# Two column chunks of wr and wi in one load, and another order of the first ten microseconds

## The chip, the core and the metric

The kernel runs on one core of one Trainium2 chip. A core has five engines that run their own instruction queues and wait for one another through semaphores: TensorE (matmuls and transposes into eight accumulator banks, in the profile PE, its weight loads PEld), VectorE (DVE), ScalarE (ACT), GpSimd (POOL) and SyncE (SP), whose queue here issues nearly all DMAs between the main memory and the on-chip memory of 128 partitions. The metric is the time of one execution on the device, in microseconds (us).

## The reference

x is 2048 x 640. It is normalised by row, xn = (x - mean) / sqrt(var + eps). Two branches of xn are summed with x:

```python
a = einsum("bsd,ed->bse", xn, wr)        # hidden DFT, 640 x 640, real part
b = einsum("bsd,ed->bse", xn, wi)        # imaginary part
y = einsum("ts,bse->bte", cr, a) - einsum("ts,bse->bte", ci, b)   # sequence DFT, 2048 x 2048
h = gelu(xn @ w1 + b1)                   # 640 -> 1536, tanh form
out = x + y + (h @ w2 + b2)              # 1536 -> 640
```

All matrices are inputs in float32, the DFT matrices too.

## The kernel before

Each matrix that goes through the TensorE is split into a high part, rounded to the type that the TensorE takes at full rate, and a low part, the rest. A product is then three matmuls, high by high, high by low, low by high (`product`, L278 to L280). `split` (L160, L161) makes the two parts: a copy on ScalarE, a subtraction on VectorE.

The rows of x are taken in four blocks of 512 (four chunks of 128 rows each). For the first block the MLP runs in twelve groups, one for each 128 columns of w1 (chunks of w1): `hidden(g)` gives 15 matmuls of 128x512 (five column chunks of x by three, L304), `gelu` and a split follow, and `output(g)` gives 15 matmuls into five banks, two groups later. The second block does the same beside the preparation of what follows; from about 180 us on blocks three and four of the MLP and then the sequence and hidden DFTs run, with sums and differences of operands that save products. The DFT matrices are turned on VectorE (32x32 transposes) after they are loaded, as the TensorE needs them the other way round.

The order of the instructions on each engine is the order in which the code is written; no scheduler changes it. A DMA of the SP queue uses one of eight semaphores in turn, so it also waits until the DMA eight places before it has landed. A tile of a pool with one buffer makes its next user wait for the readers of the last.

The front, up to the first products: x's first four chunks (0 to 3 in the code and here; the prediction counts them one to four) come by DMA. Meanwhile the TensorE runs ten warm-up matmuls on zeros (L676). Chunks 0 and 2 get their means on VectorE and are centred there (`center`, L705). Chunk 1 is summed (L699) and centred (L716) on ScalarE. Chunk 3 is summed on ScalarE and centred on VectorE, in two pieces, the first two column chunks and the other three. The centred chunks are turned on the TensorE (`transpose_x`, L693), five transposes each, into five banks, one for each column chunk of x; chunks 0 and 1 first, then one more warm-up, then chunks 2 and 3 by column chunk. Then the five banks are split into `XT` (in the profile xtt), the moving operand, the first chunk of w1 having been split in two pieces (L728, L729) before. The scale of the normalisation is made later and applied after the products: the TensorE spreads it over the columns with four transposes (`spread`, L764) one product into the third group.

wr and wi are needed in seven combinations of their column chunks, which are made, split and stored to memory (the wit tiles) long before their use. Column chunk j of one of them is the 32 columns j of each quarter of its columns, so a load of it (`load_w`, L388, four DMAs) has rows of 32 floats. `turn_w` (L396) turns a chunk; `put_w` splits and stores. `prep_w` does this in three steps for each chunk, beside the groups of the second block: chunk 0 in groups 0 to 2, chunk 1 in groups 3 to 5, the others from a later stage on. The names in the profile are wraw (as loaded), wt (turned), wst (split).

Of the kernel before, what the change touches and what calls it, by code (L numbers as in the profile page):

```python
# [16 lines left out]
Q = 4  # L17
B = 32
EPS = 1e-5
NWARM = 10  # L20
TAIL = 4
ASIDE = 1
PADL = 8
# [3 lines left out]
def kernel(  # L27
# [78 lines left out]
    def bank(k):  # L106
        return banks[:, k]
# [140 lines left out]
    def load_w1(i, eng=nc.sync, cuts=(0, ND)):  # L248
        if i >= NF:
            return  # L250
        t = early.tile([P, ND, P], F32, tag="w1r", bufs=3, name=f"w1r{i}")
        w1r[i] = t
        v = w1.rearrange("(q c i) f -> q i c f", q=Q, i=B)
        for c0, c1 in zip(cuts, cuts[1:]):
            for q in range(Q):
                eng.dma_start(t[q * B : (q + 1) * B, c0:c1], v[q, :, c0:c1, i * P : (i + 1) * P])
# [30 lines left out]
    def unit(g):  # L287
        return g if g < NF else LATE[g % NF]

    def hidden(g, aside=None):  # L290
# [4 lines left out]
        if g == 0:  # L295
            steps = FIRST
        if g == 1:

            steps.sort(key=lambda s: s[1] == 2)
        for n, (j, k) in enumerate(steps):  # L300
            if aside and n == ASIDE:
                aside()
            a, b = kinds[k]
            nc.tensor.matmul(  # L304
                acc, W1[i][:, a, j * P : (j + 1) * P], XT[j][:, b], start=n == 0, stop=n == len(steps) - 1
            )
        return acc


    FIRST = [(0, 0), (0, 2), (1, 0), (1, 2), (0, 1), (2, 0), (2, 2), (1, 1), (3, 0), (3, 2)]  # L310
    FIRST += [(2, 1), (4, 0), (4, 2), (3, 1), (4, 1)]

    def gelu(g, acc, fill=lambda k: None):

# [60 lines left out]

    A = {}

    def load_w(m, j):

        if A["w"]:  # L380
            t = A["w"].tile([P, EB, B], F32, tag=f"wraw{m}", bufs=1, name=f"wraw{m}_{j}")
        else:
            t = A["wz"][:, m].rearrange("p (e b) -> p e b", b=B)
        A["wraw", m] = t
        v = (wr, wi)[m].rearrange("(n r) d -> r n d", r=B)
        for q in range(Q):
            s0 = q * DQ + j * B
            nc.sync.dma_start(t[q * B : (q + 1) * B], v[:, :, s0 : s0 + B])  # L388

    def turn_w(m, j):  # L390
        if A["w"]:
            t = A["w"].tile([P, D], F32, tag=f"wt{m}", bufs=1, name=f"wt{m}_{j}")
        else:
            t = A["wz"][:, 2 + m]
        A["wt", m] = t
        nc.vector.transpose(  # L396
            t.rearrange("p (c q i) -> p q c i", q=Q, i=B),
            A.pop(("wraw", m)).rearrange("p (q c) i -> p q c i", q=Q),
        )
# [20 lines left out]
    def prep_w(s):  # L420

        j, k = divmod(s, 3)
        if j >= ND:
            return
        if k == 0:
            turn_w(0, j)
            turn_w(1, j)
            if j + 1 < ND and j != WEARLY - 1:
                load_w(0, j + 1)
                load_w(1, j + 1)  # L430
        (r1, r2, r4), (i1, i2, i4) = (
            (A["wt", m][:, : 2 * P], A["wt", m][:, 2 * P : 4 * P], A["wt", m][:, 4 * P :]) for m in range(2)
        )
# [12 lines left out]
        if k == 2:  # L446
            put_w(3, j, r1)
            put_w(4, j, i1)
            put_w(5, j, r2)
# [215 lines left out]
    nc.vector.memset(zeros, 0.0)  # L665
    warm = whole["as"][:, :TB]
    nc.vector.tensor_copy(warm, zeros)  # L667

    nc.scalar.activation(eps[:, 1:2], eps[:, 0:1], AF.Sqrt)
    load_w1(0, cuts=(0, 2, ND))  # L670
    load_w1(1, cuts=(0, 2, ND))

    wacc = bank(0)

    def warm_up():
        nc.tensor.matmul(wacc, warm[:, :P], warm, start=True, stop=True)  # L676

    for k in range(NWARM):
        warm_up()
    load_w1(2)  # L680
    load_w2(0)
    nc.sync.dma_start(b1c, b1.rearrange("(i p) -> p i", p=P))
    load_w2(1)
# [7 lines left out]
    def transpose_x(c, j0, j1):  # L691
        for j in range(j0, j1):
            nc.tensor.transpose(tacc[j][:, c * P : (c + 1) * P], xp[:, c, j * P : (j + 1) * P], ident)  # L693
# [32 lines left out]
    for lo, hi in ((0, 2 * P), (2 * P, D)):  # L726
        h, l = (W1[0][:, k, lo:hi] for k in range(2))
        nc.scalar.activation(h, first_w1[:, lo:hi], AF.Copy)  # L728
        nc.vector.tensor_tensor(l, first_w1[:, lo:hi], h.bitcast(F32), op=ALU.subtract)  # L729
    transpose_x(0, 0, ND)  # L730
# [202 lines left out]
    def first_block(i):  # L933

        if i < 2:
            ln_apply(2 * i)
            ln_apply(2 * i + 1)
            load_x(4 + 2 * i)
            load_x(5 + 2 * i)
        if 2 <= i < 6:  # L940
            ln_stats(4 + i - 2)
        if i == 6:
            ln_scale(4, 4)
            for c in range(4, 8):
# [24 lines left out]

    def open_tw():  # L970
        A["es"].close()
# [12 lines left out]
    def second_block(i):  # L984
# [816 lines left out]
```

## Time and profile before

| | |
|---|---|
| median of three runs | 851.04 us (850.51 to 851.35) |
| the profiled execution | 850.46 us, span 848.7 us |
| TensorE busy | 841.7 us of the span, 3707 matmuls |
| VectorE busy | 666.8 us |
| ScalarE busy | 356.0 us |
| first warm-up matmul | 1.91 us after the span's start |
| first product of the first block | 9.66 us |
| first matmul of the third group | 16.7 us |
| output 0 | 20.59 us |

A row of the profile's order of time has the start, the length, the engine, the line, the operation, what it writes and reads, the shape and the count of merged instructions; in brackets stands how long the engine had been idle before and who ended that. "SPq" and "ACTq" are DMAs issued by these queues; their length is that of the issue, not of the transfer. A row of the chain has the start, the length and what ran. A matmul's length in the profile includes its way through the array, so 0.39 us stands for a product of which one is started every 0.227 us. A row of waits has the engine and line that waited, whom it waited for, the sum, the count and the longest.

### The profile page before, as it was taken

To read this page: it belongs to the slowest core of one execution; us is meant where nothing else is said; L and a number is where in the kernel's file an instruction comes from. 1 tells how busy PE (TensorE), PEld (TensorE's weight loads), DVE (VectorE), ACT (ScalarE), POOL (GpSimd) and SP (SyncE) were. 2 spreads that over 40 slices of the span, in tenths; PEclk is the share of its full clock that TensorE was granted. 3 is DMA by queue.
4 is the path that set the end of the run, shared out by engine and by line. 5 is a ranking of instruction groups with operands and counts; after the bars stand their busy time and mean duration, and the time that the engine had idled before them with its cause. 6 is when DMAs were issued, how large, how long until landed. Compare 5 with 4: busy or idle time off the path is not lost.

```text
span 848.7 us, 10340 instructions
## 1 busy us (share of the span) xinstructions
PE 841.7 (99%) x3707; PEld 695.2 (82%) x3707; DVE 666.8 (79%) x841; ACT 356.0 (42%) x499; POOL 48.9 (6%) x70
## 2 busy tenths in 40 slices
PE   9999999999999999999999999999999999999997
PEld 7888888878888888888888888888888888888886
DVE  6665766776758888779988887889967898885687
ACT  7454534456665555343444344232323433223241
POOL 0000311031221400000000000000000000000001
PEclk9999999999999999999999999999999999999999
DMA  6667699837679989858644679663865779705464
GB/s 182 192 184 188 159 228 252 193 87 189 202 245 355 358 186 174 173 132 188 152 137 111 162 229 289 151 150 98 205 168 169 253 191 229 306 19 180 124 172 108
DMA packets 207491, 158.45 MB, mean 187 GB/s; under 512 B 81040, under 2 KB 180880, under 8 KB 206928
## 3 DMA queue, kind: packets, MB, share of 16 engines
q1 hardware_dynamic: 198752, 135.25, 62.7%
q0 software_dynamic: 4144, 21.24, 6.3%
q10 hardware_dynamic: 4544, 1.31, 0.6%
q8 instruction: 29, 0.48, 0.3%
q14 instruction: 22, 0.18, 0.1%
HBM read 114.76 MB, written 42.99 MB: 186 GB/s over the span
## 4 chain that ended last, share of the span: by engine, by line
PE 99%; DVE 0%; issue 0%
PE banks L278 29%; PE banks L279 29%; PE banks L280 29%; PE banks L304 10%; PE banks L676 1%; PE banks L693 0%; PE banks L336 0%; PE banks L339 0%; PE banks L337 0%; DVE yo L1766 0%; DVE zeros L665 0%; DVE as L667 0%; PE banks L764 0%
## 5 line engine op out<-in xcount | busy, mean ns | idle before, releaser
L278 PE MATMUL banks<-as,xab 128*128 128x512 f32 x411 | 159.9, 389 | 0.0
L280 PE MATMUL banks<-as,xab 128*128 128x512 f32 x411 | 159.9, 389 | 0.0
L279 PE MATMUL banks<-as,xab 128*128 128x512 f32 x411 | 159.9, 389 | 0.0
L160 ACT ACTIVATE as<-r 128x1024 fp32r<-128x1024 f32 x80 | 85.0, 1062 | 178.1 <-PE banks L280 149.7
L161 DVE TENSOR_TENSOR as<-r,as 128x1024 fp32r<-128x1024 f32 x80 | 97.2, 1216 | 41.5 <-ACT as L160 41.5
L278 PEld LDWEIGHTS banks<-as,xab 128*128 128x128 f32 x411 | 77.1, 188 | 16.1
L279 PEld LDWEIGHTS banks<-as,xab 128*128 128x128 f32 x411 | 77.1, 188 | 16.0
L280 PEld LDWEIGHTS banks<-as,xab 128*128 128x128 f32 x411 | 77.1, 188 | 16.0
L278 PE MATMUL banks<-as,xc 128*128 128x512 f32 x224 | 87.1, 389 | 0.0
L279 PE MATMUL banks<-as,xc 128*128 128x512 f32 x224 | 87.1, 389 | 0.0
L280 PE MATMUL banks<-as,xc 128*128 128x512 f32 x224 | 87.1, 389 | 0.0
L160 ACT ACTIVATE as<-rt 128x1024 fp32r<-128x1024 f32 x32 | 34.0, 1062 | 70.5 <-PE banks L280 62.5
L304 PE MATMUL banks<-xtt,xab 128*128 128x512 f32 x240 | 57.1, 391 | 0.0
L304 PEld LDWEIGHTS banks<-xtt,xab 128*128 128x128 f32 x240 | 44.7, 188 | 9.8 <-ACT xtt L160 0.4
L278 PEld LDWEIGHTS banks<-as,xc 128*128 128x128 f32 x224 | 42.0, 188 | 8.8
L279 PEld LDWEIGHTS banks<-as,xc 128*128 128x128 f32 x224 | 42.0, 188 | 8.7
L280 PEld LDWEIGHTS banks<-as,xc 128*128 128x128 f32 x224 | 42.0, 188 | 8.7
L161 DVE TENSOR_TENSOR as<-rt,as 128x1024 fp32r<-128x1024 f32 x32 | 38.8, 1211 | 5.3 <-ACT as L160 5.3
L160 ACT ACTIVATE as<-u 128x1024 fp32r<-128x1024 f32 (+1 forms) x24 | 22.1, 920 | 48.2 <-PE banks L280 48.2
L512 DVE STREAM_TRANSPOSE r<-raw 128x1024 f32<-128x1024 f32 x32 | 39.5, 1240 | 3.1 <-PE banks L280 2.6
L161 DVE TENSOR_TENSOR as<-u,as 128x1024 fp32r<-128x1024 f32 (+1 forms) x24 | 24.9, 1042 | 18.8 <-ACT as L160 18.8
L512 DVE STREAM_TRANSPOSE rt<-raw 128x1024 f32<-128x1024 f32 x32 | 38.8, 1230 | 0.9 <-PE banks L280 0.8
(352 smaller groups left out, 1618.5 us busy)
## 6 DMA issues: line engine op xcount, KB each, us to landing
raw<-in_A_dft_seq_re_dram SPq DMA_DIRECT2D x64, 256.0 KB, 5.6
raw<-in_A_dft_seq_im_dram SPq DMA_DIRECT2D x64, 256.0 KB, 5.0
ws<-wit SPq DMA_DIRECT2D x15, 384.0 KB, 5.4
xs<-x SPq DMA_DIRECT2D x64, 80.0 KB, 1.8
xo<-in_A_x_dram SPq DMA_DIRECT2D x16, 320.0 KB, 6.7
xab<-wit SPq DMA_DIRECT2D x13, 384.0 KB, 4.2
wit<-wstp POOLq DMA_DIRECT2D x12, 384.0 KB, 3.7
x<-in_A_x_dram SPq DMA_DIRECT2D x14, 320.0 KB, 4.4
```

Source lines behind the costliest of these rows:

```text
L160: nc.scalar.activation(h, s, AF.Copy)
L161: nc.vector.tensor_tensor(l, s, h.bitcast(F32), op=ALU.subtract)
L278: nc.tensor.matmul(acc, wh, mh, start=first, stop=False, skip_group_check=goes_on)
L279: nc.tensor.matmul(acc, wh, ml, start=False, stop=False, skip_group_check=goes_on)
L280: nc.tensor.matmul(acc, wl, mh, start=False, stop=last, skip_group_check=goes_on)
L304: nc.tensor.matmul(acc, W1[i][:, a, j * P : (j + 1) * P], XT[j][:, b], start=n == 0, stop=n == len(steps) - 1)
L512: nc.vector.transpose(held(pieces[g][2], u).rearrange("p c (n i) -> p c n i", i=B), r.rearrange("p n (c i) -> p c n i", i=B))
L676: nc.tensor.matmul(wacc, warm[:, :P], warm, start=True, stop=True)
```

## The change

There are two parts.

In the front, the warm-ups become thirteen matmuls of 128x128 on zeros in plain float32, so the cast of the zeros goes and the memset shrinks to 128 columns. The first two column chunks of x's chunk 3 are centred on ScalarE, right after the sum; chunk 2 is centred in two pieces. The split of w1's first 256 columns stands between the pieces, the split of the other 384 behind the first two copies of `XT`. Seven of chunk 2's and 3's ten transposes are done ahead of the first two products, the last three behind them. The first and second groups' products are mixed at their seam (`first_two`), and the order within each is another. w1's chunk 1 comes by four DMAs instead of eight, chunk 2 by eight instead of four.

wr's and wi's column chunks 0 and 1 are loaded together (`load_two`), with rows of 64 floats: the first 16 of wi's 20 row blocks go to a tile that lies idle (ZT), in the first block's group 10, before the stores of x that stand there; the other four of wi's and all of wr's follow at the place where chunk 0 was loaded. `turn_two` turns a chunk, wi's in three pieces and wr's in two, chunk 1 at the start of group 3 of the second block, ahead of the turning of z. The loads of chunk 1 at the end of group 0 go.

TensorE, from its first instruction to the third group, before (L676 are warm-ups, L693 transposes of x, L304 products of groups one and two, and with xab_123 of the third; L764 the spread):

```order
L676 MATMUL banks<-as 128x512 x10
L693 MATMUL banks<-ident,xp 128x128 x10
L676 MATMUL banks<-as 128x512
L693 MATMUL banks<-ident,xp 128x128 x10
L304 MATMUL banks<-xtt,xab_122 128x512 x30
L304 MATMUL banks<-xtt,xab_123 128x512
L764 MATMUL banks<-ident,ab 128x128 x4
```

The same after:

```order
L714 MATMUL banks<-zeros 128x128 x13
L731 MATMUL banks<-ident,xp 128x128 x10
L714 MATMUL banks<-zeros 128x128
L731 MATMUL banks<-ident,xp 128x128 x7
L304 MATMUL banks<-xtt,xab_122 128x512 x2
L731 MATMUL banks<-ident,xp 128x128 x3
L304 MATMUL banks<-xtt,xab_122 128x512 x28
L322 MATMUL banks<-xtt,xab_123 128x512
L810 MATMUL banks<-ident,ab 128x128 x4
```

Three transposes have moved behind the first two products, and the warm-ups have another shape and count.

ScalarE from the sum of chunk 3 (x_120) on, before (xab_122 holds w1's chunks 0 and 1 split, w1r their raw tiles):

```order
L699 ACTIVATE ab,mv<-x_120 128x640
L728 ACTIVATE xab_122<-w1r_139 128x256
L728 ACTIVATE xab_122<-w1r_139 128x384
L160 ACTIVATE xtt<-banks 128x512 x5
L160 ACTIVATE xab_122<-w1r_148 128x640
```

And after:

```order
L737 ACTIVATE ab,mv<-x_120 128x640
L767 ACTIVATE xp<-x_120,mv 128x4x2x32
L764 ACTIVATE xab_122<-w1r_138 128x256
L160 ACTIVATE xtt<-banks 128x512 x2
L764 ACTIVATE xab_122<-w1r_138 128x384
L160 ACTIVATE xtt<-banks 128x512 x3
L160 ACTIVATE xab_122<-w1r_147 128x640
```

The centring (L767) has come in ahead of w1, and w1's 384 columns stand behind two of the copies.

The SP queue from the load of xo on, 87 to 140 us, before (xs is x normalised, stored for the DFTs; ys and xo belong to the first block's output; z is the second block's operand; the last number of wraw's shape is the floats in a row):

```order
L363 DMA xo_842<-in_A_x_dram 32x16x160 x4
L203 DMA xs<-x_657 32x640 x4
...
L178 DMA x_879<-in_A_x_dram 128x640
L388 DMA wraw_0_919<-in_A_dft_hid_re_dram 32x20x32 x4
L388 DMA wraw_0_924<-in_A_dft_hid_im_dram 32x20x32 x4
L930 DMA ys_60<-xo_842 2048x1x64
L930 DMA ys_61<-xo_842 2048x1x64
L930 DMA ys_62<-xo_842 2048x1x32
L234 DMA z_1018<-xs 32x16x160 x4
L388 DMA wraw_1_1033<-in_A_dft_hid_re_dram 32x20x32 x4
L388 DMA wraw_1_1038<-in_A_dft_hid_im_dram 32x20x32 x4
L203 DMA xs<-x_873 32x640 x4
```

And after:

```order
L381 DMA xo_845<-in_A_x_dram 32x16x160 x4
L404 DMA zt<-in_A_dft_hid_im_dram 32x16x64 x4
L203 DMA xs<-x_660 32x640 x4
...
L178 DMA x_886<-in_A_x_dram 128x640
L404 DMA wrest<-in_A_dft_hid_im_dram 32x4x64 x4
L404 DMA wraw<-in_A_dft_hid_re_dram 32x10x64 x8
L976 DMA ys_60<-xo_845 2048x1x64
L976 DMA ys_61<-xo_845 2048x1x64
L976 DMA ys_62<-xo_845 2048x1x32
L234 DMA z_1029<-xs 32x16x160 x4
L203 DMA xs<-x_880 32x640 x4
```

Four loads have gone ahead of the stores of x, twelve stand where eight stood, and the eight behind the load of z are gone.

```diff
-NWARM = 10
+NWARM = 13
...
+    def first_two():
+        kinds = ((0, 0), (0, 1), (1, 0))
+        second = sorted(((j, k) for j in range(ND) for k in range(3)), key=lambda s: s[1])
+        order = [(0, s) for s in FIRST[:13]] + [(1, s) for s in second[:2]]
+        order += [(0, FIRST[13]), (1, second[2]), (0, FIRST[14])] + [(1, s) for s in second[3:]]
+        for n, (g, (j, k)) in enumerate(order):
+            if n == 2:
+                transpose_x(3, 2, ND)
+                for e in range(2, ND):
+                    split(XT[e][:, 0], XT[e][:, 1], tacc[e])
+                prep_w1(1)
...
+    def load_two(m, k0=0):
+        v = (wr, wi)[m].rearrange("(n r) d -> r n d", r=B)
+        for t, n0, n1 in TWO[m][k0:]:
+            for q in range(Q):
+                nc.sync.dma_start(t[q * B : (q + 1) * B], v[:, n0:n1, q * DQ : q * DQ + 2 * B])
+    def turn_two(m, j):
+        t = A["wt", m] = A["w"].tile([P, D], F32, tag=f"wt{m}", bufs=1, name=f"wt{m}_{j}")
...
-        if k == 0:
+        if k == 0 and j == 0:
+            turn_two(1, j)
+            turn_two(0, j)
+        if k == 0 and j >= WEARLY:
             turn_w(0, j)
             turn_w(1, j)
-            if j + 1 < ND and j != WEARLY - 1:
+            if j + 1 < ND:
...
-    nc.vector.memset(zeros, 0.0)
-    warm = whole["as"][:, :TB]
-    nc.vector.tensor_copy(warm, zeros)
+    nc.vector.memset(zeros[:, :P], 0.0)
...
-    load_w1(1, cuts=(0, 2, ND))
+    load_w1(1)
...
-        nc.tensor.matmul(wacc, warm[:, :P], warm, start=True, stop=True)
+        nc.tensor.matmul(wacc[:, :P], zeros[:, :P], zeros[:, :P], start=True, stop=True)
...
-    load_w1(2)
+    load_w1(2, cuts=(0, 2, ND))
...
-    center(2, ALU.subtract, MV[:, 2, 0:1])
     sum_on_act(3)
-    center(3, ALU.add, MV[:, 3, 5:6], 0, 2)
-    center(3, ALU.add, MV[:, 3, 5:6], 2, ND)
...
+    nc.scalar.activation(
+        chunked(xp[:, 3])[:, :, :2],
+        xt[3].rearrange("p (q c i) -> p q c i", q=Q, i=B)[:, :, :2],
+        AF.Identity,
+        bias=MV[:, 3, 5:6],
+    )
+    center(2, ALU.subtract, MV[:, 2, 0:1], 0, 2)
+    center(2, ALU.subtract, MV[:, 2, 0:1], 2, ND)
+    split_first(0, 2 * P)
+    center(3, ALU.add, MV[:, 3, 5:6], 2, ND)
     transpose_x(0, 0, ND)
     transpose_x(1, 0, ND)
     warm_up()
-    for j0, j1 in ((0, 2), (2, ND)):
-        transpose_x(2, j0, j1)
-        transpose_x(3, j0, j1)
-    for j in range(ND):
+    transpose_x(2, 0, 1)
+    transpose_x(3, 0, 2)
+    transpose_x(2, 1, ND)
+    for j in range(2):
         split(XT[j][:, 0], XT[j][:, 1], tacc[j])
+    split_first(2 * P, D)
...
-    acc0 = hidden(0)
-    prep_w1(1)
-    acc1 = hidden(1)
+    acc0, acc1 = first_two()
...
             load_xo(0)
+            TWO[1] = [(ZT.rearrange("p a (e b) -> p (a e) b", b=2 * B), 0, WCUT)]
+            load_two(1)
...
-        load_w(0, 0)
-        load_w(1, 0)
+        t = A["w"].tile([P, EB, 2 * B], F32, name="wraw")
+        TWO[0] = [(t[:, : EB // 2], 0, EB // 2), (t[:, EB // 2 :], EB // 2, EB)]
+        TWO[1].append((A["w"].tile([P, EB - WCUT, 2 * B], F32, name="wrest"), WCUT, EB))
+        load_two(1, 1)
+        load_two(0)
...
         if i == 3:
+            turn_two(1, 1)
+            turn_two(0, 1)
```

More of the change, by code (lines that the diff above doesn't have):

```diff
@@ L288, in unit @@
         return g if g < NF else LATE[g % NF]
+    def first_two():
[9 more added lines that the diff above has]
+                prep_w1(1)
+            a, b = kinds[k]
+            ends = FIRST if g == 0 else second
+            nc.tensor.matmul(
+                bank(g),
+                W1[g][:, a, j * P : (j + 1) * P],
+                XT[j][:, b],
+                start=(j, k) == ends[0],
+                stop=(j, k) == ends[-1],
+            )
+        return bank(0), bank(1)
     def hidden(g, aside=None):
@@ L294, in hidden @@
         steps = [(j, k) for j in range(ND) for k in range(3)]
[L295 to L299, printed above, removed]
         for n, (j, k) in enumerate(steps):
@@ L307, in hidden @@
         return acc
-    FIRST = [(0, 0), (0, 2), (1, 0), (1, 2), (0, 1), (2, 0), (2, 2), (1, 1), (3, 0), (3, 2)]
-    FIRST += [(2, 1), (4, 0), (4, 2), (3, 1), (4, 1)]
+    FIRST = [(0, 0), (0, 2), (1, 0), (1, 2), (0, 1), (2, 0), (1, 1), (3, 0), (2, 2), (3, 2)]
+    FIRST += [(4, 0), (4, 2), (2, 1), (3, 1), (4, 1)]
     def gelu(g, acc, fill=lambda k: None):
@@ L376 @@
     A = {}
+    TWO = {}
+    WCUT = TB // B
+    def load_two(m, k0=0):
[5 more added lines that the diff above has]
+        t = A["wt", m] = A["w"].tile([P, D], F32, tag=f"wt{m}", bufs=1, name=f"wt{m}_{j}")
+        places = t.rearrange("p (c q i) -> p q c i", q=Q, i=B)
+        for src, n0, n1 in TWO[m]:
+            q0, q1 = -(-n0 // ND), n1 // ND
+            s = src[:, :, j * B : (j + 1) * B]
+            if q0 < q1:
+                nc.vector.transpose(
+                    places[:, q0:q1], s[:, q0 * ND - n0 : q1 * ND - n0].rearrange("p (q c) i -> p q c i", c=ND)
+                )
+            if n0 % ND:
+                nc.vector.transpose(places[:, q0 - 1, n0 % ND :], s[:, : q0 * ND - n0])
+            if n1 % ND:
+                nc.vector.transpose(places[:, q1, : n1 % ND], s[:, q1 * ND - n0 :])
     def load_w(m, j):
[L380 to L383, printed above, removed]
+        t = A["wz"][:, m].rearrange("p (e b) -> p e b", b=B)
         A["wraw", m] = t
@@ L390, in turn_w @@
     def turn_w(m, j):
[L391 to L395, printed above, removed]
+        t = A["wt", m] = A["wz"][:, 2 + m]
         nc.vector.transpose(
@@ L721, with split_first @@
     ln_stats(2)
-    center(2, ALU.subtract, MV[:, 2, 0:1])
     sum_on_act(3)
-    center(3, ALU.add, MV[:, 3, 5:6], 0, 2)
-    center(3, ALU.add, MV[:, 3, 5:6], 2, ND)
-    for lo, hi in ((0, 2 * P), (2 * P, D)):
+    def split_first(lo, hi):
         h, l = (W1[0][:, k, lo:hi] for k in range(2))
@@ L729 @@
         nc.vector.tensor_tensor(l, first_w1[:, lo:hi], h.bitcast(F32), op=ALU.subtract)
+    nc.scalar.activation(
[3 more added lines that the diff above has]
+        bias=MV[:, 3, 5:6],
+    )
+    center(2, ALU.subtract, MV[:, 2, 0:1], 0, 2)
+    center(2, ALU.subtract, MV[:, 2, 0:1], 2, ND)
+    split_first(0, 2 * P)
+    center(3, ALU.add, MV[:, 3, 5:6], 2, ND)
     transpose_x(0, 0, ND)
```

## The prediction

> **What bounds the kernel now.** I read the page's busy times first, then the chain that ended last, then the waits of the TensorE, and only then the first 21 us, instruction by instruction.
>
> ```profile
> span 848.7 us, 10340 instructions
> PE 841.7 (99%) x3707; PEld 695.2 (82%) x3707; DVE 666.8 (79%) x841; ACT 356.0 (42%) x499; POOL 48.9 (6%) x70
> PE 99%; DVE 0%; issue 0%
> ```
>
> A busy share of 99% could hide slow matmuls, so the same is asked by stretch (columns: stretch, length, PE busy with its count, weight loads, DVE, ACT, POOL, granted clock, DMA share, GB/s), and of the waits of the weight loads, which stand ahead of each matmul:
>
> ```profile
> 17.30:179.40 162.10, 162.10 (x718) 134.19 (x717) 111.54 (x208) 78.94 (x133) 14.77 (x20) 1.00 0.74 189
> 187.60:843.60 656.00, 655.96 (x2894) 542.75 (x2892) 536.09 (x599) 260.15 (x335) 26.25 (x38) 1.00 0.69 188
> PEld banks L278 <- ACT banks L857: 0.3, 1, 0.3
> PEld banks L278 <- DVE banks L452: 0.3, 1, 0.3
> PEld banks L279 <- DVE xtt L161: 0.3, 1, 0.3
> ```
>
> From 17.3 us on, the TensorE streams at 656.0/2894 = 0.227 us for each 128x512 product, with three waits of 0.3 us between 179 and 188 us and none elsewhere. The number of products is the same after the change. So the time is (when the stream starts) + (products) x 0.227, and a change can win only in the front, or lose there, or by making a new wait. The front, from the chain:
>
> ```profile
> 0.91 0.50 DVE zeros L665
> 1.43 0.44 DVE as L667
> 1.91 4.63 PE banks L676 x10
> 6.54 1.87 PE banks L693 x10
> 8.40 0.24 PE banks L676
> 8.64 1.09 PE banks L693 x10
> 9.73 7.38 PE banks L304 x31
> 17.12 0.44 PE banks L764 x4
> ```
>
> Three things are to be seen. Ten warm-up products take about 4.5 us (0.43 to 0.45 each, where a later one takes 0.227): the TensorE runs at half speed at first, although the granted clock of every stretch reads 1.00. Ten transposes take 1.87 us the first time and 1.09 the second; seven or eight at twice 0.109 and the rest at 0.109 make 1.87, so the speed doubles at about 7.9 us, 6.0 us after the first warm-up. And 31 products take 7.38 us where 31 x 0.227 = 7.03: 0.35 us of stalls. A product that starts 0.8 us earlier and no stall at all would be worth 1.2 us; 0.2%, about what a measurement of this kernel can tell from no change, is 1.7 us.
>
> **The change, part by part: the front.** Who releases the first product, at 9.66 in the order of time (the chain counts it from 9.73), is seen on ScalarE and VectorE:
>
> ```profile
> 6.56 0.74 ACT L699 ACTIVATE ab<-x 128x640 f32<-128x640 f32 x1 [0.15 <-DMA x<-in_A_x_dram]
> 7.20 0.19 ACT L699 ACTIVATION_READ_ACCUMULATOR ab<-x 128x1 f32 x1
> 7.30 0.40 ACT L728 ACTIVATE xab<-w1r 128x256 fp32r<-128x256 f32 x1
> 8.47 0.53 ACT L728 ACTIVATE xab<-w1r 128x384 fp32r<-128x384 f32 x1 [0.77 <-DMA w1r<-in_B_w_dram]
> 9.01 1.09 ACT L160 ACTIVATE xtt<-banks 128x512 fp32r<-128x512 f32 x2
> 7.38 1.15 DVE L705 TENSOR_SCALAR xp<-x,mv 128x640 f32<-128x640 f32 x3
> 8.44 0.42 DVE L729 TENSOR_TENSOR xab<-w1r,xab 128x256 fp32r<-128x256 f32 x1
> 9.66 7.46 PE L304 MATMUL banks<-xtt,xab 128*128 128x512 f32 x31
> ```
>
> Before: chunk three's centring and both halves of chunk four's run on VectorE from 7.38 to 8.53; the last ten transposes run from 8.6 on (chain); the first copy out of the banks starts at 9.01 on ScalarE, which until 8.99 also splits 384 columns of w1; 0.60 later it is done and the first product runs.
>
> After, step by step.
> (1) Warm-ups. One memset of 128 columns takes the place of a memset of 512 and a cast. No row has it on VectorE; it lies between 0.10 and the 0.48 of the 512 columns; I take 0.2, nearer the short end because the tile is a quarter. The first warm-up moves from 1.91 to about 1.16 (1.06 to 1.45).
> (2) A 128x128 product in plain float32 is in no row. Its price lies between that of the float32 transposes of the shape (0.21 at half speed) and twice that of a 128x512 product (0.86). I take 0.43, the price of the products that it replaces, which are the nearest in kind. Then 13 end between 6.3 and 6.9, depending on when the speed doubles; chunk one is centred at 6.28 (5.72 plus 0.56), so nothing is lost up to 6.4 and 0.5 at most.
>
> ```profile
> 5.72 0.56 DVE L705 TENSOR_SCALAR xp<-x,mv 128x640 f32<-128x640 f32 x1
> ```
>
> The Trainium skill, "FP8 and Floating Point Precision", TensorE Precision Notes, says that true FP32 is four passes through the array; by it the price would be 4 x 128 = 512 columns, as taken; no run here shows it.
> (3) Chunk four's first two column chunks are centred on ScalarE, right after the sum: 7.39 + 0.04 + about 0.43 (between the 0.40 of a 128x256 copy and 0.45, the same for a strided one) = 7.86, against 8.20 on VectorE. The w1 copy of 256 columns goes behind it, 7.77 to 8.17; that is hidden, since the copy out of the banks waits for the transposes.
> (4) At full speed ten transposes and a warm-up end at about 7.9, chunk three's first transpose and chunk four's follow by 8.03, land by 8.19, the copy out starts at 8.23 and the first product at 8.88: 0.77 earlier.
> (5) Three transposes of chunk four now stand behind the first two products: 3 x 0.109 = +0.33. They wait for the last centring on VectorE, which comes behind the 256-column split (8.2 to 8.54) and ends at 8.95, before the second product does. The 384-column split of w1 (0.53) moves behind the second copy, on ScalarE and VectorE both; it ends at 9.7, and copies three to five follow some 0.5 apart (two that overlap take 1.09), each ahead of its product.
> (6) w1's second chunk comes in four DMAs instead of eight. The SP queue issues four in 1.84, so the last goes out at 8.45 instead of 10.34 and lands 1.8 us later (the third row is the landing of the second group), or 2.0 for the larger piece, at 10.5; ScalarE gets to it at 11.2 instead of 12.42:
>
> ```profile
> 7.04 1.84 SPq L256 DMA_DIRECT2D w1r<-in_B_w_dram  x4
> 8.92 1.84 SPq L256 DMA_DIRECT2D w1r<-in_B_w_dram  x4
> DMA to landing us min/median/max: 1.8/1.8/1.9
> 12.42 0.74 ACT L160 ACTIVATE xab<-w1r 128x640 fp32r<-128x640 f32 x1 [0.86 <-DMA w1r<-in_B_w_dram]
> ```
>
> That wait costs 0.1 of the 0.35 us of stalls; with the two groups of products mixed I count 0.1 more back and keep 0.2 for the start behind the transposes: -0.1. w1's third chunk is cut in eight instead, its last DMA is the twelfth of the same twelve and goes out when it did.
> The sum at an early doubling of the speed: -0.77 + 0.33 - 0.1 = about -0.5. If the speed doubles 6.0 us after the first warm-up, as in the row, that is 7.2: half of the ten transposes run slow (+0.11 each), the warm-ups end 0.4 later, and the sum is about 0. If it doubles at 7.9, at the same moment as before, the ten transposes end at 8.5 and the sum is +0.4. I take the middle of the first two, -0.3.
>
> What is late next: ScalarE's chain behind it ends in the table load, gelu and the copy that output 0 waits for.
>
> ```profile
> 17.35 1.28 ACT L760 ACT_TABLE_LOAD   x1
> 19.58 0.63 ACT L326 ACTIVATE hs<-ab 128x512 fp32r<-128x512 f32 x1
> 20.59 0.39 PE L336 MATMUL banks<-hs,rt 128*128 128x512 f32 x1
> 12.72 0.43 SPq L263 DMA_DIRECT2D w2r<-in_B_w_dram  x1
> DMA to landing us min/median/max: 3.4/3.4/3.4
> ```
>
> The copy ends at 20.21 with 0.38 us to spare. The chain moves earlier with ScalarE until it meets w2's first chunk, which lands at 16.1 (12.72 + 3.4), some 0.5 before ScalarE takes it up ahead of the table load. So the chain can come 0.5 earlier and has 0.4 to spare: a gain of up to 0.8 passes through.
>
> **The change, part by part: wr and wi.** Sixteen DMAs of 128-byte rows for chunks 0 and 1 become sixteen of 256-byte rows; four go out ahead, twelve where eight did, none where the second eight did; four VectorE transposes become ten.
>
> ```profile
> 86.65 1.92 SPq L363 DMA_DIRECT2D xo<-in_A_x_dram  x4
> 95.00 7.36 SPq L203 DMA_DIRECT2D xs<-x  x16
> 104.77 4.32 SPq L388 DMA_DIRECT2D wraw<-in_A_dft_hid_re_dram  x4
> 124.12 6.00 SPq L388 DMA_DIRECT2D wraw<-in_A_dft_hid_re_dram  x4
> 114.22 0.85 DVE L396 STREAM_TRANSPOSE wt<-wraw 128x640 f32<-128x640 f32 x1 [1.68 <-DMA wraw<-in_A_dft_hid_im_dram]
> 116.33 0.63 ACT L326 ACTIVATE hs<-ab 128x512 fp32r<-128x512 f32 x1
> ```
>
> The first four fill a gap of the SP queue (88.6 to 95.0). The queue is then freed of the second eight, whose first four alone take 6.0 us from 124 on, so the stores of x and the z load behind them come earlier. Ten transposes of the same elements cost what four cost, 4 x 0.85, plus six more starts, at 0.1 to 0.2 each: 0.6 to 1.2 us on an engine that is busy 111.5 of 162.1 us. If the raw tiles land later than at 114.2 (VectorE waited 1.68 us for the last of them), VectorE and ScalarE hold up the gelu behind them (116.33 here). What it makes is used two groups on, each group 6.8 us of TensorE, so some 11 us may be lost before a product waits. On the path: 0, with 0 to +0.5 as its bounds.
>
> The sum is -0.3 us against the profiled execution's 850.46. That lies 0.6 under the median of the three runs, 851.04, whose spread is 0.84; I put the difference on the median: 850.7.
>
> **The rivals.**
> R1, the other side: the float32 warm-up costs twice as much. From 0.64 us each it decides, since 13 then outlast the centring. At 0.85 (0.45 at full speed) they end at 9.1 to 10.3, the first product comes at 11.9 to 13, and the kernel is 2.2 to 3.8 us slower: 853.2 to 854.8. For it speaks that a float32 transpose of 128 columns (0.109) costs almost half of a 512-column product (0.227), and that four times the transpose's 0.21 would be just this 0.85; against, that it is the far end of the bounds.
> R2: the warm-up costs 0.21. Then 13 end at 4.0, the TensorE idles 2.3 us, and the speed doubles only 6.0 us after the transposes start, at 12.3 or earlier: products from 9.4 on run at half speed and lose up to 1.5 us, the transposes 0.6, against 0.5 won. 0 to +1.7: 851.0 to 852.7.
> R3: the speed doubles at a moment of its own, whatever the warm-ups do; at 7.9 and later the front wins nothing: +0.1 to +0.5, 851.1 to 851.5. One trace, with the switch 6.0 us after the first product, cannot tell. The Trainium skill, "TensorE: Matmul & The Clock Gate", Part 1, has a free-running window of about 3.4 us that must be busy throughout; by it the doubling lies anywhere from 4.6 to 8.0 us, and half of these give the full -0.5, so by it the sum would be about -0.4.
> R4: wr and wi put a wait on the stream, against the 11 us: +2 to +5, 853 to 856.
> R5: the change does nothing that shows, because the stalls that leave the front come back at w2's first chunk: 850.9 to 851.2.
>
> **How the numbers follow.** Forecast, 850.1 to 851.0: 0.48. R3 and R5 together 0.22, R1 0.12, R2 0.08, R4 0.06, more than 1.7 us faster 0.04 (the three late waits, 0.5, would have to go too, and more than the front holds). Within 0.2% are the forecast, R3, R5 and most of R2: 0.76; slower, R1, R4 and the rest of R2: 0.20. The range 849.9 to 852.6 leaves out R1, most of R4 and the far faster end, under 2 in 10.
>
> **What the profile after would show.** (1) a first warm-up near 1.16 and a 0.43 spacing; 0.85 is R1, a gap before the transposes R2. (3), (4) ScalarE's centring at 7.4 and a first product near 8.9. (5) three transposes after two products, and no wait there. (6) the second chunk's copy at 11.2. The four transposes ahead of output 0 (17.12 in the chain) near 16.8 and output 0 near 20.3. From there on 0.227 us for each product. The prediction is wrong if any wait of the TensorE stands between 85 and 180 us, or if output 0 starts after 22.

## The result, and the profile after

The changed kernel takes 852.67 us (median; its runs lie between 850.44 and 855.37), the kernel before 850.68 us in the same comparison (850.29 to 852.14). The ratio is 1.0021, with a 95% interval of 1.0014 to 1.0028: slower by 1.8 us. The prediction was 850.7 us, with a range of 849.9 to 852.6; the median lies just above it. The profiled execution of the changed kernel took 852.5 us, its span is 850.7 us. Each kernel has one profiled execution, and what its rows show is that execution, not the median.

The front did nearly what the prediction said. VectorE, ScalarE and TensorE of the changed kernel, in the order of time (start, length, engine, line, operation, what it writes and reads, count):

```profile
0.82 0.17 DVE L705 MEMSET zeros<- 128x128 f32 x1 [0.82 <-PEq L1840]
```

```profile
7.50 0.51 ACT L767 ACTIVATE xp<-x,mv 128x256 f32<-128x256 f32 x1
7.92 0.40 ACT L764 ACTIVATE xab<-w1r 128x256 fp32r<-128x256 f32 x1
8.43 1.09 ACT L160 ACTIVATE xtt<-banks 128x512 fp32r<-128x512 f32 x2
```

```profile
1.04 5.40 PE L714 MATMUL banks<-zeros 128*128 128x128 f32 x26 [1.04 <-DVE zeros L705]
6.40 1.28 PE L731 MATMUL banks<-ident,xp 128*128 128x128 f32 x10
7.52 0.39 PE L714 MATMUL banks<-zeros 128*128 128x128 f32 x2
7.94 1.00 PE L731 MATMUL banks<-ident,xp 128*128 128x128 f32 x7
9.08 0.73 PE L304 MATMUL banks<-xtt,xab 128*128 128x512 f32 x2
9.65 0.49 PE L731 MATMUL banks<-ident,xp 128*128 128x128 f32 x3
...
20.33 0.39 PE L354 MATMUL banks<-hs,rt 128*128 128x512 f32 x1
```

The first product starts at 9.08 us (9.66 before), output 0 at 20.33 (20.59): a gain of 0.26 us, where -0.3 was predicted. The same front varies between executions: in the nine profiled executions that have the changed front (this one and eight runs below), output 0 starts at 20.04 to 20.69 us, with a median of 20.29. One detail in these rows matters below: thirteen warm-up matmuls are 26 records (instructions of the profile), and the fourteenth is two. A 128x128 matmul in plain float32 stands as two matmuls in the TensorE's program, 0.21 us each at half speed. So the TensorE executes 3724 matmul records, 17 more than before.

The loss lies later. The waits of the weight loads, and the busy time by stretch (columns as in the prediction), after:

```profile
PEld banks L278 <- ACT hs L344: 1.3, 1, 1.3
PEld banks L279 <- DVE hs L346: 0.9, 1, 0.9
...
PEld banks L322 <- DVE xab L161: 0.4, 1, 0.4
```

```profile
140.00:160.00 20.00, 18.59 (x82) 14.81 (x81) 12.93 (x28) 8.02 (x17) 3.76 (x7) 1.00 0.71 210
200.00:843.60 643.60, 643.60 (x2842) 532.88 (x2841) 530.52 (x590) 253.68 (x325) 26.20 (x38) 1.00 0.69 189
```

and the first of these stretches before:

```profile
140.00:160.00 20.00, 20.00 (x90) 16.53 (x90) 12.70 (x25) 7.92 (x17) 2.70 (x5) 1.00 0.90 251
```

Between 140 and 160 us the TensorE starts 82 products instead of 90: 8 x 0.227 = 1.8 us. It waits for `hs`, the output of a gelu, twice from 149.6 us on. ScalarE shows why that gelu is late, after:

```profile
146.72 0.42 ACT L160 ACTIVATE wst<-wt 128x256 fp32r<-128x256 f32 x1 [6.28 <-DMA wit<-wst]
147.04 0.29 ACT L453 ACTIVATE wst<-wt 128x128 fp32r<-128x128 f32 x1
148.90 0.62 ACT L160 ACTIVATE wst<-wt 128x256 fp32r<-128x256 f32 x2 [1.56 <-DMA wit<-wst]
149.42 0.67 ACT L340 ACTIVATE ab<-banks,b1c 128x512 f32<-128x512 f32 x1
```

The same four operations before:

```profile
141.88 0.42 ACT L160 ACTIVATE wst<-wt 128x256 fp32r<-128x256 f32 x1 [2.00 <-DMA wit<-wst]
142.21 0.29 ACT L416 ACTIVATE wst<-wt 128x128 fp32r<-128x128 f32 x1
143.33 0.62 ACT L160 ACTIVATE wst<-wt 128x256 fp32r<-128x256 f32 x2 [0.83 <-DVE wt L452]
143.85 0.67 ACT L322 ACTIVATE ab<-banks,b1c 128x512 f32<-128x512 f32 x1
```

The staging tile `wst` is filled anew in every step of `prep_w`, so ScalarE must wait until the store of the last step (`wit<-wst`) has landed, and the gelu stands behind that wait in ScalarE's queue. It is 5.6 us later than before. Two things can make it so: the preparation as a whole is late, or its stores land late. GpSimd's queue, which issues these stores, shows both, after:

```profile
117.96 1.31 POOL L455 DMA_DIRECT2D wit<-wst  x2 [11.67 <-DVE wst L161]
...
141.17 1.08 POOL L455 DMA_DIRECT2D wit<-wst  x2 [7.26 <-DVE wst L161]
148.09 0.54 POOL L455 DMA_DIRECT2D wit<-wst  x1 [5.84 <-DVE wst L454]
```

and before:

```profile
115.89 1.32 POOL L418 DMA_DIRECT2D wit<-wst  x2 [11.22 <-DVE wst L161]
...
138.27 1.14 POOL L418 DMA_DIRECT2D wit<-wst  x2 [7.08 <-DVE wst L161]
143.25 0.54 POOL L418 DMA_DIRECT2D wit<-wst  x1 [3.84 <-DVE wst L417]
```

The first store goes out 2.1 us later, and the store after the pair at 141.17 waits 5.84 us where 3.84 were. The experiments separate the two.

### The profile page after: what moved, and what is told of

Same layout as the page of the kernel before. It is cut to its first block, busy times and chain, and to the rows that moved or that the text cites. A ratio compares the mean times of both kernels' runs of the same rounds, so it can differ in the third digit from the quotient of the medians.

```text
span 850.7 us, 10378 instructions
## 1 busy us (share of the span) xinstructions
PE 842.9 (99%) x3724; PEld 696.5 (82%) x3724; DVE 666.1 (78%) x846; ACT 356.2 (42%) x500; POOL 49.0 (6%) x70
## 4 chain that ended last, share of the span: by engine, by line
PE 88%; DMA 4%; DVE 3%; ACT 2%; issue 2%; SPq 1%; POOL 0%; ACTq 0%; DVEq 0%; POOLq 0%
PE banks L279 27%; PE banks L278 27%; PE banks L280 27%; PE banks L322 3%; DMA wit<-wst 2%; DMA z<-xs 1%; PE banks L304 1%; DMA x<-in_A_x_dram 1%; PE banks L714 1%; SPq L203 0%; DVE zt L238 0%; ACT ab L340 0%; DVE st L185 0%; DMA wraw<-in_A_dft_hid_re_dram 0%; DVE xtt L161 0%
## 5 line engine op out<-in xcount | busy, mean ns | idle before, releaser
L322 PE MATMUL banks<-xtt,xab 128*128 128x512 f32 x210 | 50.3, 390 | 0.0
L322 PEld LDWEIGHTS banks<-xtt,xab 128*128 128x128 f32 x210 | 39.3, 188 | 8.5 <-DVE xab L161 0.4
```

The source lines that it names most:

```text
L322: nc.tensor.matmul(acc, W1[i][:, a, j * P : (j + 1) * P], XT[j][:, b], start=n == 0, stop=n == len(steps) - 1)
```

## The experiments

All are timed against the kernel before on the same chip. Of the theories, A says that the stores of wit land slowly, because the SP queue, freed of eight loads, now runs the loads of z and rq beside them; B says that wr's data come late; C says that the earlier front puts later work out of step. D was formed after the first four runs and is told below; E, formed after the first seven, says that more small warm-ups cost by themselves, in proportion to their number. The profiled executions of e1 (854.29 us) and e5 (853.56) are the longest of eleven, and that of e3 (850.35) is the shortest, so their waits don't add up to the medians. (`load_rq` loads w1's columns for a later stage; z(1), z(3) are turned blocks of the normalised x.)

| run | what it is | us | ratio to before, 95% interval |
|---|---|---|---|
| e1 | changed front alone | 852.34 | 1.0017, 1.0008 to 1.0026 |
| e2 | changed wr and wi alone | 850.88 | 1.0002, 0.9993 to 1.0010 |
| e3 | whole change, z(3) and rq held back | 851.63 | 1.0009, 1.0000 to 1.0018 |
| e4 | whole change, stores of wit on SP's queue | 863.54 | 1.0150, 1.0137 to 1.0164 |
| e5 | before, warm-ups cut into 17 more records | 852.38 | 1.0016, 1.0007 to 1.0025 |
| e6 | whole change, one-record warm-ups | 851.15 | 1.0007, 0.9998 to 1.0016 |
| e7 | changed front alone, one-record warm-ups | 850.63 | 0.9997, 0.9988 to 1.0005 |
| e8 | before, 8 more records | 851.06 | 1.0005, 0.9996 to 1.0013 |
| e9 | before, 50 more records | 853.78 | 1.0026, 1.0014 to 1.0038 |
| e10 | whole change, one-record warm-ups, z(3) and rq held back | 850.35 | 0.9992, 0.9983 to 1.0000 |
| e11 | e10 again | 850.33 | 0.9996, 0.9988 to 1.0005 |
| e12 | e10 without the change to wr and wi | 850.41 | 0.9999, 0.9990 to 1.0008 |

### Each part alone

e1 takes only the hunks of the diff on the front, e2 only those on wr and wi.

> The changed front alone, with wr and wi loaded and turned as before. Theory A (the staging tile: in the whole change the stores of wit land in 7 us instead of 3.6, since the freed SP queue lets the loads of z and rq run beside them, ScalarE waits for those stores, and the gelu stands behind it) and theory B (wr's data come later as one large load, so every step of the preparation is late, whatever the stores take) both expect the front's own gain and nothing else: ratio 0.9995 to 0.9998, about 850.3 to 850.5 us, output 0 near 20.3 us, no gap of the TensorE at 149 to 152 us. Theory C (the shifted front itself puts the later groups out of step) expects slower than before, by 0.1 to 0.3%.

> The change to wr and wi alone, with the front of before. Theories A and B expect the whole loss: ratio 1.002 to 1.003, 852.5 to 853.3 us, a gap of 1.5 to 2.5 us of the TensorE at 149 to 152 us, and single runs spread over some 4 us. Theory C expects no loss: within 0.05% of before.

Theories A and B fell as explanations of the whole: the front alone carries the loss, and wr and wi alone cost nothing that shows. In e2 the two stores of wit near 139 us take 6.3 us to land, as long as in the whole change (before: 3.9), so what A describes does happen; but its first store goes out at 115.73 us, as before, and the TensorE does not wait. In e1 wr and wi are as before, and the first store goes out late all the same. Its stores near 141 us land in 4.2 us, though, and it loses its time not at 149 us but mostly in a wait of 2.1 us at 180.6 us. GpSimd's queue in e1:

```profile
118.34 1.31 POOL L436 DMA_DIRECT2D wit<-wst  x2 [11.80 <-DVE wst L161]
```

Theory C had the right part, but not how 0.26 us earlier could make a store 2.4 us later.

### Holding the other loads back, or moving the stores

e3 puts the loads of z(3) and rq behind `prep_w(4)`:

```diff
@@ second_block, i == 3
-            load_z(3)
@@ open_xf
-        load_rq(0)
@@ main loop, behind prep_w(k)
+            if i == 4:
+                load_z(3)
+                load_rq(0)
@@ load_z
+        if t == 3:
+            nc.vector.memset(z[:, 0, :1], 0.0)
```

> The whole change, but the loads of z(3) and of the first rq are held back on SP until VectorE has done prep_w(4) (one element a partition is set in z's tile there, and the loads stand behind it). Theory A: the stores of wit issued near 141 us land in about 3.6 us again, ScalarE's put at 146.7 waits at most 2 us, the gap at 149 to 152 is under 0.3 us, and the time is 850.3 to 850.8 us (ratio 0.9993 to 1.0002); z and rq are wanted only two and three groups later, so they cost nothing. Theory B: the stores land sooner but the steps are late all the same, the gap stays over 1 us: 851.5 to 852.7 us.

e4 changes the queue of the stores:

```diff
-        nc.gpsimd.dma_start(wits[w][j], t[:, :, :n].bitcast(F32))
+        (nc.sync if A["w"] else nc.gpsimd).dma_start(wits[w][j], t[:, :, :n].bitcast(F32))
```

> The whole change, but the early stores of wit (six steps, 14 stores) are issued on SP's queue in place of POOL's. Theory A: if what is slow is the landing of POOL's stores beside other loads, the wait of ScalarE falls to under 1 us and the time to 850.3 to 850.8 us, unless a store stands in SP's queue behind a load of 4 to 9 us wait, in which case some of the gap stays (851 to 852). Theory B: the gap at 149 to 152 stays over 1 us, 852 to 853.

e3 removed the gap at 149 us, but the median came down only by 1 us, to 851.63. In its profiled execution the first store still goes out late, at 117.44 us, the stores near 140 us land in 2.8 us, and a wait of 0.8 us stands at 179 us; that execution took 850.35 us, so a late first store alone need not cost time. Where the longer executions of e3 lose theirs is in no trace. e4 lost 13 us. Each store then stands in the SP queue until VectorE has filled the tile, and the loads stand behind it; SP's queue in e4:

```profile
124.17 9.83 SPq L455 DMA_DIRECT2D wit<-wst  x4
137.54 8.35 SPq L203 DMA_DIRECT2D xs<-x  x16
145.99 1.39 SPq L455 DMA_DIRECT2D wit<-wst  x3
```

So four stores hold the queue for 9.8 us. This run tells nothing of the cause, only that GpSimd's queue is the better place.

### What the front moves

Going back from e1's first store (118.34, before 115.89), each step is late because of the one ahead: the data of wr, the loads of x, the load of xo, and first of all z(1), whose transposition on VectorE (L238) opens the chain. Before, and e1:

```profile
78.63 0.71 DVE L238 STREAM_TRANSPOSE zt<-z 128x512 f32<-128x512 f32 x1 [0.60 <-DMA z<-xs]
```

```profile
80.06 0.71 DVE L238 STREAM_TRANSPOSE zt<-z 128x512 f32<-128x512 f32 x1 [1.66 <-DMA z<-xs]
```

z(1) is issued only 0.4 us later in e1, but lands 1.4 us later. In the profiles of the change, e1, e3 and e4, with the front of the change, z is transposed at 79.4 to 80.1 us, in those of the kernel before and e2 at 78.6 and 78.5. What is new in z's load is a single packet. The DMA queues between 71.0 and 77.7 us, in which z's 2048 packets move (queue, kind: packets, MB, share of 16 engines); before, and after:

```profile
q1 hardware_dynamic: 2167, 1.45, 110.6%
```

```profile
q1 hardware_dynamic: 2151, 1.45, 106.7%
q8 instruction: 1, 0.02, 1.3%
```

Queue q8 moves 29 pieces of 16 KB in the whole execution, each as one packet: 29 x 16384 bytes over 2 x 3724 records (a matmul and its weight load) is 64 bytes each. The Trainium skill ("Trainium Architecture — The Big Picture", The software stack) states this size for an instruction, so the trace agrees; the same section has the instruction streams moved to the engines when the kernel is loaded, and there the trace differs, with these 29 pieces during the execution. The size and the spacing say that it is the TensorE's program, fetched while it runs: one piece for each 128 products, 128 x 0.227 = 29 us; counted in the traces, the TensorE starts 127 matmuls between two fetches in the mean, before and after. Before, the fetches begin at 21.6, 49.8, 80.5 and 108.4 us; with 17 more matmul records ahead of them they come earlier (after: 18.9, 45.1, 75.2, so by 2.7, 4.7 and 5.2 us, where 17 x 0.227 would be 3.9). 1.3% of 16 engines over 6.7 us is 1.4 us of one engine. Of z's packets 99% have ended by 77.45 us before and by 77.74 after, but the last one ends at 77.68 and 78.64. That fits one engine that lags behind the other fifteen, the load having landed only when it is through; the trace doesn't name the engine of a packet. That is theory D; e5 and e6 test it from both sides.

e5 is the kernel before, with its warm-ups cut finer, in bfloat16, and nothing else; e6 and e7 give the change one-record warm-ups of the same length:

```diff
@@ e5, against the kernel before
-NWARM = 10
+NWARM = 27
-        nc.tensor.matmul(wacc, warm[:, :P], warm, start=True, stop=True)
+        low = warm.bitcast(BF16)
+        nc.tensor.matmul(wacc[:, :190], low[:, :P], low[:, :190], start=True, stop=True)
@@ e6 against the changed kernel, e7 against e1
-        nc.tensor.matmul(wacc[:, :P], zeros[:, :P], zeros[:, :P], start=True, stop=True)
+        low = zeros[:, :P].bitcast(BF16)
+        nc.tensor.matmul(
+            wacc.rearrange("p (a b) -> p a b", a=4), low[:, :P], low[:, None, :P].broadcast_to([P, 4, P]), start=True, stop=True
+        )
```

> The kernel before with nothing changed but its ten warm-ups cut into 27 of 190 bfloat16 columns, which fill about the same time: 17 more matmul records ahead of the transposes, as many as the changed kernel has. Theory D (TensorE's program is fetched in pieces of 16 KB by one DMA engine; 17 more matmuls at the start move each fetch 3 to 5 us earlier, from 80.5 us to about 77 us, into the load of z(1) at 71 to 77.7 us; that engine lags, z(1) lands over 1 us late, and xo, x, wraw and the preparation of wit follow late) expects the whole loss without any change of the front's work or of wr and wi: ratio 1.0010 to 1.0025, 851.6 to 852.9 us, first transposed z at 79.4 to 80.1 us (78.6 before), first store of wit at 117.5 to 118.5 us (115.9 before). Theory C (the earlier first product puts the groups out of step with their loads) expects no loss: within 0.05% of before, z at 78.6 us.

> The whole change, but the warm-ups are of bfloat16 and 512 columns, one record each instead of two, with about the same time each: 14 records in place of 28, so 3 more than before instead of 17. Theory D expects the loss gone: 850.2 to 850.8 us (ratio 0.9993 to 1.0003), fetches near 21, 49 and 80 us, z(1) transposed at 78.2 to 78.6 us, first store of wit near 115.7 us, no gap at 149 to 152 us. Theory C, and any theory by which wr and wi or the shifted front lose the time, expects 852 to 853 us.

> The changed front alone (wr and wi as before), with the same one-record warm-ups. Theory D expects the front's own gain and nothing else: 850.1 to 850.6 us (ratio 0.9992 to 0.9999), against 852.3 us with the two-record warm-ups. Theory C expects 852 us again.

e5 loses 1.6 us although its first product is even earlier than before (9.49 us). Its DMA queues between 71.0 and 77.7 us, VectorE and GpSimd:

```profile
q1 hardware_dynamic: 2137, 1.43, 106.4%
q8 instruction: 1, 0.02, 1.2%
```

```profile
80.27 0.71 DVE L239 STREAM_TRANSPOSE zt<-z 128x512 f32<-128x512 f32 x1 [2.15 <-DMA z<-xs]
```

```profile
118.31 1.31 POOL L419 DMA_DIRECT2D wit<-wst  x2 [11.59 <-DVE wst L162]
```

It has the same late chain, and its main wait is e1's, not that of the whole change: 2.0 us at 180.9 us, with smaller ones at 136 and 157 us. The chain that ended last leads from that wait back to z (four of its rows; the chain of the kernel before is 99% TensorE):

```profile
71.62 8.53 DMA z<-xs
...
118.31 4.06 DMA wit<-wst
...
151.06 8.10 DMA rq<-in_B_w_dram
...
182.24 0.59 ACT banks L859
```

In the changed kernel the chain passes through the same load of z and then through the late stores of wit, to the waits from 149.6 us on:

```profile
71.51 8.20 DMA z<-xs
...
141.71 7.11 DMA wit<-wst
```

So the late preparation can reach the TensorE in two ways: through the stores of wit and ScalarE near 150 us, or through the later load of rq and VectorE's work on it at 181 us. A small wait near 31 us for the split of w1 (`xab`) stands in the changed kernel, e1, e5 and e6; it is not settled.

e7, the front without the moved fetches, is at 850.63 us: 1.7 us faster than e1, level with before. (A wait of 1.0 us at 179 us is left in its profiled execution, which took 850.88.) Its fetches begin at 21.2, 48.6 and 79.5 us, and VectorE and GpSimd are back:

```profile
78.12 0.71 DVE L239 STREAM_TRANSPOSE zt<-z 128x512 f32<-128x512 f32 x1 [0.53 <-DMA z<-xs]
```

```profile
115.45 1.31 POOL L437 DMA_DIRECT2D wit<-wst  x2 [11.25 <-DVE wst L162]
```

e6 won about 1.2 of the 1.8 us that the change had lost (ratio 1.0007 for 1.0021), not all: 851.15 lies above what D expected. Its z is on time (78.43), but its first store goes out at 116.82 us, and a gap of 0.5 us is left at 149.7 us, where the stores take 6.5 us to land. There what A describes counts.

### How many records, and where the fetch falls

> The kernel before with its ten warm-ups cut into 18 of 284 bfloat16 columns: 8 more records instead of 17. In the run with 17 more the fetch moved 4.1 us, 0.24 us a record. Theory D (it matters which load a fetch falls into): the fetch lies at about 78.6 us, behind the last packet of z(1) at 77.7 us, so z(1) is transposed at 78.4 to 78.8 us as before, the first store of wit stands at 115.5 to 116.5 us, and the time is 850.4 to 851.1 us. Theory E (more small warm-ups cost by themselves, in proportion): half of the loss with 17, 851.4 to 851.8 us.

> The kernel before with its ten warm-ups cut into 60 of 85 bfloat16 columns: 50 more records. Theory D: the fetch moves by some 12 us, to about 68.5 us, ahead of the load of z(1) (71 to 77.7 us), so z(1) is transposed at 78.4 to 78.9 us again; the next fetch goes from 108.4 to about 96.4 us, out of the load of x, so the first statistics stand near 105.8 us; 850.3 to 851.3 us, so the loss is not monotonic in the count. Theory E: three times the loss with 17 more, over 854 us.

e8 (18 warm-ups of 284 columns) came out as D said: fetch at 79.4 us, z at 78.57, first store at 115.71, and 851.06 us, which is not told apart from before. e9 (60 of 85 columns) did not: 853.78 us. Its fetch is indeed gone from the load of z, but it now lies at 65.9 us, in the stores of x (`xs`) that z's load reads from. SP's queue, before and e9:

```profile
61.27 7.36 SPq L203 DMA_DIRECT2D xs<-x  x16
70.08 1.91 SPq L234 DMA_DIRECT2D z<-xs  x4
```

```profile
61.37 8.87 SPq L204 DMA_DIRECT2D xs<-x  x16
71.69 1.91 SPq L235 DMA_DIRECT2D z<-xs  x4
```

The sixteen stores take 1.5 us longer (the fetch took 1.63), because each of SP's DMAs waits for the one eight places before it. z is transposed at 80.19 us, and the next fetch (96.4 us) does the same to the next sixteen stores, 8.10 us for 7.36. So in these traces a fetch among the stores of x or in z's load delays the chain by 0.7 to 1.5 us, and one at 79 to 80.5 us, behind z's last packet, does not; what it would cost elsewhere in the chain wasn't tried. D expected 850.3 to 851.3 us for e9 and missed: it had not asked what the fetch would meet in the new place. By times alone e9 lies just under theory E's "over 854", and e8 lies between before and e5. A cost in proportion to the count is spoken against only by the rows of e8 and e9, not excluded by their medians.

### Both causes removed

> The whole change with one-record warm-ups (6 of 10 parts of the loss gone in the run with these alone: 851.15 us) and with the loads of z(3) and rq held back behind prep_w(4). If what is left is the wait of ScalarE for the stores of wit beside those loads (theory A, now for the rest), no gap at 149 to 152 us and 850.2 to 850.6 us, ratio 0.9993 to 0.9999, the fastest of all; if wr's and wi's rest of loss has another cause, 851.0 to 851.3 us again.

> The kernel of the run before once more (the whole change, one-record warm-ups, z(3) and rq held back), for a second interval: 850.2 to 850.6 us, ratio 0.9992 to 0.9998 if its gain is real.

> The same without the change to wr and wi: the changed front, one-record warm-ups, z(3) and rq held back, wr and wi in 128-byte rows as before. If the change to wr and wi is worth nothing once its loads no longer meet the stores of wit, 850.2 to 850.6 us, level with the run beside it; if the fewer rows gain, this one is slower by over 0.2 us; if wr and wi cost by themselves, faster by over 0.2 us.

The kernel with both edits has the lowest medians of all, 850.35 us (e10) and 850.33 when run again (e11); no product waits at 149 us, and the stores between 136 and 143 us land in 2.6 us in e10. e11's first store goes out at 116.81 us, as late as e6's, and costs nothing, which speaks for the landing of the stores as the rest of e6's loss. By the medians the two lie 0.4 and 0.25 us under the kernel before; the part that their intervals share, 0.9988 to 1.0000, is level with it or up to 1 us faster. e12, with wr and wi as they were, is at 850.41 us beside e11's 850.33: the 256-byte rows are worth nothing that shows, and cost nothing once the loads that they let through are held back.

## Why the prediction was wrong

Point by point, by its own steps:

- Steps (1) to (6), right in kind and near in size, but for the records in (2). First warm-up 1.04 us (1.16); float32 warm-up 2 x 0.213 = 0.43 us (0.43); centring 7.50 to 8.0 us (7.43 to 7.86); first product 9.08 (8.88); w1's second chunk copied at 11.41 (11.2); sum -0.26 us (-0.3). e7, without the disturbance, has a ratio of 0.9997, which agrees but can't be told from no gain. The four passes of the Trainium skill ("FP8 and Floating Point Precision", TensorE Precision Notes) agree with the measured 0.43 us; that they come as two records it does not say.
- That the sum came out so near is in part luck. The first product won 0.58 of the 0.77 us. The speed doubled early, at 5.7 us, a case for which the prediction's sum was -0.5; -0.3 was a middle between that and a second case whose terms as written (five slow transposes, warm-ups 0.4 us later) make about +0.4, not "about 0". The 6.0 us from the first warm-up to full speed are no constant either: in e2, with the front of before, the ten warm-ups take 4.25 us (4.63 before), the ten transposes after them 1.28 (1.98), and output 0 starts at 20.59 us in both.
- The step that failed is (2). It priced the float32 warm-up by its time and put everything else about it at nothing, as did "The number of products is the same after the change." The warm-ups are 28 records instead of 11, 17 more in the TensorE's program. That moved its fetches, the third one by 5.2 us into z(1)'s load. e5 shows that 17 more records alone cost 1.6 us in the kernel before, e7 that without them the front costs nothing that shows.
- The second failure is the slack in the part on wr and wi: "some 11 us may be lost before a product waits", counted from one gelu to its use two groups on. The gelu stands in ScalarE's queue behind copies into `wst`, which wait for stores. Before, ScalarE already waited 11.4 us for them in five waits between 115 and 160 us (17.5 us in seven after). A preparation 2.1 us late, with stores that take 6.3 us, used up the slack in the changed kernel.
- That part's price, 0 to +0.5 us, is not contradicted: by the medians e2 +0.1 us, e6 against e7 +0.5 (by their ratios 0.9), e11 against e12 -0.1, none of them certain. The freed SP queue did bring the z load earlier, as was said (140.40 us, before 144.90); that it would meet the stores of wit was not.
- R4 had the place and nearly the size (a wait on the stream, 853 to 856) but the wrong cause, and too small a chance, 0.06. R1, R2 and R3 were about the price of the warm-ups and the clock, and did not happen: a warm-up took 0.43 us, nothing idles ahead of the transposes, and the spacing of the warm-ups shows full speed from 5.7 us on, 4.7 us after the first. What R3 says of the moment, that it is not set by the warm-ups alone, has e2 on its side. In e7 it comes about 2.7 us after the first warm-up, earlier than the 3.4 us of which R3 speaks: thirteen of them take 4.29 us, 0.427 us apart at half speed and 0.216 at full.
- "The prediction is wrong if any wait of the TensorE stands between 85 and 180 us" was the right thing to watch: the waits of the changed kernel stand from 149.6 us on.

Not settled: why the same kernel's executions spread over 5 us after the change, where most of those before lie within 1 us. That the moved fetch and the late stores put several waits near their edge is argued, not shown. Nor do the traces say why the late preparation costs nothing in some executions (e3's, with z at 79.39 us) and 2 us or more in others.

## What to carry to other kernels

Count instruction records as well as microseconds when a change adds cheap work on the TensorE: the program is itself loaded while it runs, and 17 records more at the start decide which data transfer a later fetch delays. When a change that should be neutral loses time far from where it was made, compare the landings of the DMAs in between, and then try the kernel before with only its instruction count changed. Slack behind an in-order queue is what the wait of its slowest neighbour leaves, not the distance to the consumer.

## What was not expected of the hardware

- The TensorE's program comes in pieces of 16 KB (q8), one for each 128 matmuls; each is one packet, which takes 0.9 to 1.9 us in the changed kernel. The load of z(1), four DMAs of 320 KB, takes at most 7.0 us to land before, and 8.1 to 8.5 us in the change, e1 and e5, where it meets one.
- A float32 128x128 matmul is two records of 0.213 us at half speed, a bfloat16 one of 190 columns is one record (27 in 3.80 us in e5, part of them at half speed).
- Stores of 384 KB issued by GpSimd land in 2.6 us with the loads of z and rq held back (e10), in 3.9 beside the stores of x (before), and in 6.3 beside the loads of z and rq (e2).
